# Reordering the hand-written schedule around the second batch's scores, reads and turns

## The chip, the cores and the metric

The kernel runs on one core of a Trainium2 chip. The metric is the device time of one execution in microseconds. TensorE (PE) multiplies matrices into PSUM; VectorE (DVE), ScalarE (ACT) and GpSimd (POOL) do the element-wise work; SyncE (SP) only issues transfers. Lines of the profile name these engines by the short forms, and L12 is line 12 of the kernel.

## The reference

Two blocks follow one another. The first is a cross attention between a long sequence `x` (8 batches, 8 heads, 512 rows, 64 columns) and 32 state rows per head, in both directions. The second takes the 544 rows of each batch, 512 wide, adds the real part of a two-dimensional Fourier transform, normalises the rows and runs a two-layer network over them with a residual. Some 5,000 matrix rows pass through the two layers (512 to 2048 to 512).

```python
def _attn_ref(x, state):
    scores = scale * np.matmul(x, state.transpose(0, 1, 3, 2))
    a = np.exp(scores - max); a /= a.sum(-1)      # 512 x 32 per head
    xread = np.matmul(a, state)
    scores2 = scale * np.matmul(state, x.transpose(0, 1, 3, 2))
    a2 = softmax(scores2)                         # 32 x 512 per head
    sread = np.matmul(a2, x)
    return np.concatenate([xread, sread], axis=2)

def _moe_ref(x, w_ch1, w_ch2):
    mixed = np.real(np.fft.fft(np.fft.fft(x, axis=1), axis=2))
    u = x + mixed
    un = (u - mean(u)) / np.sqrt(var(u) + 1e-06)
    return u + np.maximum(un @ w_ch1, 0.0) @ w_ch2
```

(Softmax and mean are shortened here.)

## The kernel before

**Order of work.** The engines run in parallel, but each goes through its own instructions in the order in which the program issues them. Nothing reorders them: the program text is the schedule. For batches 0 and 1 that order is written out by hand, call by call (lines 1111 to 1239); from batch 2 on, a function `weave` spreads lists of steps over a stage by fractions. The change touches the hand-written part alone.

**Steps of one batch.** A batch b passes through these, and the schedule interleaves several batches:

- `attend(b)` gives the attention. *Scores* (`scores(i)`, L422, then the exponential E on ScalarE, L427) are made twice, for two halves of the rows. *Turned scores* (`turn_scores(g)`, L434, copied to ET on ScalarE, L435) follow. In the schedule these four are `s1[0..3]` for batch 1, `s2[0..3]` for batch 2, `s3[0..3]` for batch 3.
- *Reads* follow: `r1` for batch 1, `R` for batch 2. R[0] is the first row read, with a copy XT of 32 rows made on GpSimd (L501); R[1] folds that copy on GpSimd (`fold_low`, `fold_low_again`); R[2], R[4] and R[6] are the other row reads (`xread`, L447 on TensorE, then a reciprocal and a multiply on VectorE, L455 and L456); R[3] is the per-head read (`sread_by_head`, L467 on TensorE, L470 and L474 on VectorE). L474 writes the rows that the copy XT is made from. The row reads share a PSUM buffer, psX, of which there is one. R[6] to R[8] go on to the folds on VectorE that feed the transform.
- `transform(b)` gives the Fourier part: `over_s` over the rows (L774, copied to G on ScalarE, L775), `over_d` over the columns (L670, L671), `add` (L675; `add_sums`, L793, for batch 0), `centre` with the statistics of each row (L337, L339) and the centred copy `ub` (L831 on ScalarE; `centre_sums`, L808 to L814, for batch 0), and `turn_u`, which turns `ub` into the tile `unT` that layer 1 reads (L842 on TensorE, L843 the copy). For b = 0 and 1 the turn runs on TensorE, for later batches by a transfer. `T` holds these steps for batch 2. There are four pieces (k, r) per batch.
- A *root* (L343, L344, GpSimd) makes the reciprocal deviation of one piece. For batches 0 and 1 roots are collected in `first_roots` and started by hand: entries 0 and 5 to 7 belong to batch 0, entries 1 to 4 to batch 1. `spread` makes the statistics of a piece of batch 0, for the root.
- `layer1(b)` multiplies by the first weights: `L` for batch 0 is 16 quarter steps (L927, four steps per column group of unT, in the order of the four turns), `L1` for batch 1 is 16 steps (L917) that each read all of unT. The activation goes to hT on ScalarE (L929, L919).
- `layer2(b)` is 16 steps of four matmuls (L982), `M` for batch 0. Four steps make one output tile; the fourth adds the residual on VectorE (`store`, L949), which needs that tile's root, and sends it out. `M1` is M[7] and those after it, so M1[1] is M[8].

**PSUM buffers.** Besides psX there are three `psQ` buffers (scores, turned scores, turned `ub`, the transform's results) and three `psF` buffers (the results of both layers). A buffer is taken in the order of the program and is free when the engine that empties it has done so.

**Other queues.** `cast_x(3)` (L148) on GpSimd converts the rows of batch 3, loaded as `xs` by SyncE (L145), and transfers turn them (`turned[3]`). GpSimd has this cast, XT's copy, the folds of low rows and the roots in one queue.

Of the kernel before, what the change touches and what calls it, by code (L numbers as in the profile page):

```python
# [30 lines left out]
def kernel(  # L31
# [8 lines left out]
    nc = tc.nc  # L40
    B, H, S, D = x.shape
# [11 lines left out]
    s_dram = nc.dram_tensor("s_dram", (B, H, Ns, D), F32, kind="Internal")  # L53
# [55 lines left out]
    def states(lo, hi):  # L109
        return stf[:, lo:hi] if lo < 3 else stl[:, lo - 3:hi - 3]  # L110

    def load_state(lo, hi, src=state):
        nc.sync.dma_start(
            out=states(lo, hi).rearrange("p b g d -> p (b g) d"),
            in_=src[lo:hi].rearrange("b (g hh) j d -> (hh j) (b g) d", hh=4),
        )
# [4 lines left out]
    def load_x(b):  # L121
        xs = xs_of[b] if b in xs_of else wk.tile([128, 4 * dm], F32, name="xs", tag="xs")
        xs_of[b] = xs
        v = xs.rearrange("p (i h d) -> p i h d", i=4, d=D)
        xb = x[b].rearrange("h s d -> s h d")
        row = v[15:32:16, 3]
        parts = [
            (v[:, 0], xb[1:129]),
            (v[:, 1], xb[144:272]),
            (v[:, 2], xb[273:401]),  # L130
            (v[32:128, 3], xb[416:512]),
            (v[0:15, 3], xb[129:144]),
            (v[16:31, 3], xb[401:416]),
            (row, xb[0:273:272]),
        ]
        if b == 0:
            for queue, n in ((nc.sync, None), (nc.scalar, 2), (nc.sync, 3), (nc.scalar, 0), (nc.sync, 4), (nc.sync, 5), (nc.sync, 6),
                             (nc.sync, 1)):
                if n is None:
                    load_state(0, 1)  # L140
                else:
                    queue.dma_start(out=parts[n][0], in_=parts[n][1])
            return
        for o, rows in parts:
            nc.sync.dma_start(out=o, in_=rows)  # L145

    def cast_x(b, copy=nc.gpsimd.tensor_copy, lo=0, hi=4):
        copy(xin_bufs[b % 2][:, lo:hi, 1:513], xs_of[b].rearrange("p (i c) -> p i c", i=4)[:, lo:hi])  # L148
# [203 lines left out]
    first_roots = []  # L352
# [5 lines left out]
    turned = {}  # L358
# [546 lines left out]
    def layer1(key):  # L905
        low = isinstance(key, tuple)
        n = 128 if low else 512
        hT = wk.tile([128, FC, n], BF16, name="hTL" if low else "hT", tag="hTL" if low else "hT", bufs=1 if low else 2)
        h_of[key] = hT
        per = 512 // n  # L910

        def step(i):
            ph = psF.tile([128, 512], F32, name="ph", tag="c")
            for f in range(per * i, per * i + per):
                o = (f % per) * n
                for c in range(DC):
                    nc.tensor.matmul(ph[:, o:o + n], lhsT=w1[:, c, f * 128:(f + 1) * 128], rhs=un_of[key][:, c, :],  # L917
                                     start=(c == 0), stop=(c == DC - 1))
            nc.scalar.activation(hT[:, per * i:per * i + per, :].rearrange("p a b -> p (a b)"), ph, AF.Relu,  # L919
                                 scale=-1.0 / 512 if key == 0 else -1.0 if key in flipped else 1.0)  # L920

        def quarter_step(i, r):
            ph = psF.tile([128, 512], F32, name="ph", tag="c")
            for f in range(4 * i, 4 * i + 4):
                o = 128 * (f % 4)
                for c in range(DC):
                    nc.tensor.matmul(ph[:, o:o + 128], lhsT=w1[:, c, f * 128:(f + 1) * 128],  # L927
                                     rhs=un_of[key][:, c, 128 * r:128 * r + 128], start=(c == 0), stop=(c == DC - 1))
            nc.scalar.activation(hT[:, 4 * i:4 * i + 4, 128 * r:128 * r + 128], ph.rearrange("p (a b) -> p a b", b=128),  # L929
                                 AF.Relu, scale=-1.0 / 512 if key == 0 else -1.0 if key in flipped else 1.0)  # L930

        if key == 0:
            return [lambda i=i, r=r: quarter_step(i, r) for r in range(4) for i in range(FC // 4)]
        return [lambda i=i: step(i) for i in range(FC // per)]
# [82 lines left out]
    begin, terms_of, low_of, out_of, keep_low, over_d, add_sums, centre_sums, turn_u, spread, done, keep_middle = transform(0)  # L1017
# [87 lines left out]
    L, M = layer1(0), layer2(0)  # L1105
    over_s1, over_d1, add1, centre1, turn_u1, done1 = transform(1)
# [20 lines left out]
    turned[2, 0]()  # L1127
    load_state(3, 4, s_dram)
    turn_u(0, 1)
    copies1[0]()  # L1130
    copies1[1]()
    copies1[2]()
    add_sums(0, 0)
    centre_sums(0, 0)
    warm(4)
    L[0]()
    s1[0]()
    s1[1]()
    L[1]()
    turn_u(0, 0)  # L1140
    add_sums(1, 1)
    add_sums(1, 0)
    L[2]()
    s1[2]()
    s1[3]()
    centre_sums(1, 1)
    L[3]()
    L[4]()
    r1[0]()
    r1[1]()  # L1150
    r1[2]()
    nc.gpsimd.tensor_copy(gate, xs_of[2].rearrange("p (i c) -> p i c", i=4)[:, :, 0])
    second_weights(2, 4)
    clear_state(4, B)
    L[5]()
    r1[4]()
    r1[3]()
    centre_sums(1, 0)
    turn_u(1, 1)
    L[6]()  # L1160
    r1[5]()
    L[7]()
    r1[6]()
    r1[7]()
    nc.gpsimd.tensor_copy(gate, XQs[1].rearrange("p (g j c) -> p g j c", g=2, j=4)[:, 1, 3, 0:4])
    for i in range(4):
# [4 lines left out]
    turned[2]()  # L1171
    load_x(3)
    turn_in_dram(4, B)
    L[8]()
    L[9]()
    turn_u(1, 0, nc.scalar.copy)
    spread(0, 1)
    state_ones(2, B)
    L[10]()
    L[11]()  # L1180
    L[12]()
    L[13]()
    over_s1(0)
    over_s1(1)
    L[14]()
    over_s1(2)
    over_s1(3)
    keep_middle()
    L[15]()
    over_d1(0)  # L1190
    add1(0, 1)
    M[0]()
    centre1(0, 1)
    over_d1(1)
    add1(0, 0)
    M[4]()
    centre1(0, 0)
    add1(1, 1)
    M[1]()
    turn_u1(0, 1, nc.scalar.copy)  # L1200
    centre1(1, 1)
    M[5]()
    add1(1, 0)
    turn_u1(0, 0, nc.scalar.copy)
    centre1(1, 0)
    M[2]()
    M[6]()
    turn_u1(1, 1)
    done()
    first_roots[0]()  # L1210
    M[3]()
    spread(0, 0)
    turn_u1(1, 0)
    first_roots[5]()
    done1()
    l2, scores_first = M, scores_next
    for b in range(1, B + 1):
        reads_next = reads_after
        l2, l2_now = (layer2(b), [l2[7]] + l2[8:]) if b == 1 else (layer2(b) if b < B else [], l2)
        early, until, start = {2: (7, 0.25, 0.22), 3: (3, 0.13, 0.1)}.get(b, (0, 0, 0.08))  # L1220
        l2_now = l2_now + (layer2(("L", b // 4)) if b in (3, 7) else [])
        streams = [(l2_now[:early], 0, until), (l2_now[early:], until + 0.02 if early else 0, 1)]
        if b == 1:
            M1, L1, R, T, s2 = l2_now, layer1(1), reads_next, transform(2), scores_first
            scores_next, reads_after = attend(3)
            s3 = scores_next
            def spreads():
                spread(1, 1)
                spread(1, 0)
                for root in first_roots[6:8] + first_roots[1:5]:  # L1230
                    root()

            for step in (M1[0], spreads, M1[1], M1[2], s2[0], s2[1], L1[0], M1[3], s2[2], s2[3], L1[1], lambda: cast_x(3), turned[3], L1[2],
                         lambda: load_state(4, B, s_dram), lambda: load_x(4), R[0], L1[3], R[1], R[3], L1[4], R[2], L1[5], M1[4], R[4],
                         L1[6], M1[5], R[6], L1[7], R[7], L1[8], M1[6], R[8], L1[9], L1[10], M1[7], T[0], T[1], L1[11], T[2], T[3],
                         L1[12], T[4], L1[13], T[5], s3[0], L1[14], T[6], s3[1], L1[15], T[7], M1[8], T[8], s3[2], s3[3], T[9], T[10],
                         T[11], lambda: state_blocks(4, B, nc.gpsimd.tensor_copy)):
                step()
            continue
        if b < B:  # L1240
            streams.append((layer1(b), start, 1))
        if b + 1 < B:
            reads, mix = {2: ((0.1, 0.45), (0.57, 0.88)), 3: ((0.03, 0.4), (0.5, 0.86))}.get(b, ((0, 0.375), (0.47, 0.85)))
            streams.append((reads_next, *reads))
            streams.append((transform(b + 1), *mix))
        if b + 2 < B:
            scores_next, reads_after = attend(b + 2)
            streams.append(([lambda: (cast_x(b + 2), turned[b + 2]())], 0.2, 0.2))
            streams.append((scores_next, 0.5, 1))
        if b + 3 < B:  # L1250
            streams.append(([lambda: load_x(b + 3)], 0.35, 0.35))
        if b in (3, 7):
            streams.append((low_rows(b // 4), 0.02, 0.2))
            streams.append((layer1(("L", b // 4)), 0.36, 0.8))
        weave(*streams)
# [30 lines left out]
```

The softmax here doesn't subtract the row's maximum and nothing guards it: scores larger than these inputs give would overflow.

## Time and profile before

Three runs gave 302.44, 302.45 and 302.70 us (median 302.45). The profiled execution has a span of 300.8 us, with the full TensorE clock throughout.

| engine | busy us | share of the span |
|---|---|---|
| PE | 286.6 | 95% |
| PE weight loads | 164.1 | 55% |
| DVE | 176.9 | 59% |
| ACT | 139.4 | 46% |
| POOL | 90.9 | 30% |

A line of a timeline gives start, duration, engine, line, operation, what is written and read, shape and count; in brackets the idle time of the engine just before it, and what ended that. A matmul's duration is modelled and overlaps with the next; four matmuls of 128x512 start 0.86 us apart in all. The table of stretches gives busy time per engine, and in brackets the number of instructions.

### The profile page before, as it was taken

To read this page: it belongs to the slowest core of one execution; us is meant where nothing else is said; L and a number is where in the kernel's file an instruction comes from. 1 tells how busy PE (TensorE), PEld (TensorE's weight loads), DVE (VectorE), ACT (ScalarE), POOL (GpSimd) and SP (SyncE) were. 2 spreads that over 40 slices of the span, in tenths; PEclk is the share of its full clock that TensorE was granted. 3 is DMA by queue.
4 is the path that set the end of the run, shared out by engine and by line. 5 is a ranking of instruction groups with operands and counts; after the bars stand their busy time and mean duration, and the time that the engine had idled before them with its cause. 6 is when DMAs were issued, how large, how long until landed. Compare 5 with 4: busy or idle time off the path is not lost.

```text
span 300.8 us, 6004 instructions
## 1 busy us (share of the span) xinstructions
PE 286.6 (95%) x2288; PEld 164.1 (55%) x2319; DVE 176.9 (59%) x441; ACT 139.4 (46%) x260; POOL 90.9 (30%) x227
## 2 busy tenths in 40 slices
PE   5998999979899999999999999999999999999995
PEld 5788894535544555466544554455444544555443
DVE  8855888457858487645748394756568474000022
ACT  6887575626734661355433534354524433334200
POOL 6764841670391044401333032502240131000000
PEclk9999999999999999999999999999999999999999
DMA  9999983958563932585343774254332033500355
GB/s 157 198 204 191 164 147 77 202 117 161 127 150 81 208 88 72 123 163 118 85 93 89 155 142 131 46 105 89 88 79 64 35 89 86 123 13 25 95 121 135
DMA packets 110824, 34.86 MB, mean 116 GB/s; under 512 B 101980, under 2 KB 106332, under 8 KB 110796
## 3 DMA queue, kind: packets, MB, share of 16 engines
q1 hardware_dynamic: 100076, 28.72, 44.3%
q0 software_dynamic: 4224, 4.19, 8.9%
q10 hardware_dynamic: 6496, 1.57, 2.6%
q8 instruction: 18, 0.29, 0.4%
q14 instruction: 10, 0.08, 0.1%
HBM read 22.41 MB, written 14.02 MB: 121 GB/s over the span
## 4 chain that ended last, share of the span: by engine, by line
PE 70%; DVE 8%; DMA 6%; SPq 5%; POOL 4%; issue 3%; ACT 2%; POOLq 0%; DVEq 0%; ACTq 0%
PE po L982 31%; PE ph L917 30%; SPq L145 4%; DMA s_dram<-in_state_dram 3%; PE gp L774 2%; DMA gen<-s_dram 2%; POOL xin L148 1%; SPq L388 1%; PE po L974 1%; DMA r_dram<-ot 1%; PE yp L671 1%; PE yp L670 1%; DVE U L675 1%; DVE st L337 1%; PE xrp L447 1%
## 5 line engine op out<-in xcount | busy, mean ns | idle before, releaser
L982 PE MATMUL po<-w,hT 128*128 128x512 bf16 x481 | 121.3, 379 | 1.3 <-issue 0.5
L919 ACT ACTIVATE hT<-ph 128x512 bf16<-128x512 f32 x112 | 66.9, 597 | 112.9 <-PE ph L917 111.8
L917 PE MATMUL ph<-unT,w 128*128 128x512 bf16 x432 | 111.7, 379 | 0.9 <-DVE ot L949 0.3
L917 PEld LDWEIGHTS <-w 128*128 128x128 bf16 x576 | 50.3, 98 | 46.0 <-issue 0.9
L982 PEld LDWEIGHTS <-hT 128*128 128x128 bf16 x496 | 46.9, 98 | 47.6
L949 DVE SCALAR_TENSOR_TENSOR ot<-po,rstd,U 128x512 f32<-128x512 f32 (+2 forms) x33 | 24.1, 731 | 51.0 <-PE po L982 45.6
L778 POOL COPY GL<-G 128x128 bf16<-128x128 bf16 x7 | 2.0, 291 | 74.0 <-ACT G L775 74.0
L337 DVE BATCH_NORM_STATS2 st<-U 128x6 f32<-128x512 f32 x32 | 21.8, 682 | 0.1
L343 POOL TENSOR_TENSOR rstd<-mv,epst 128x1 f32<-128x1 f32 x34 | 6.8, 200 | 48.1 <-DVE mv L339 48.1
L675 DVE TENSOR_TENSOR U<-yp,XR 128x512 f32<-128x512 f32 x14 | 9.5, 681 | 20.0 <-PE yp L671 20.0
L344 POOL TENSOR_TENSOR rstd<-rstd,mhalf 128x1 f32<-128x1 f32 x34 | 19.8, 583 | 2.7
L927 PE MATMUL ph<-unT,w 128*128 128x128 bf16 x256 | 16.1, 219 | 0.3 <-DVE unT L843 0.3
L775 ACT CAST G<-gp 128x288 bf16<-128x288 f32 x28 | 12.9, 482 | 4.9 <-PE gp L774 4.9
L927 PEld LDWEIGHTS <-w 128*128 128x128 bf16 x256 | 14.9, 98 | 0.5 <-issue 0.4
L929 ACT ACTIVATE hT<-ph 128x512 bf16<-128x512 f32 x16 | 9.4, 598 | 5.1 <-PE ph L927 5.0
L148 POOL CAST xin<-xs 128x2048 bf16<-128x2048 f32 (+1 forms) x9 | 11.7, 1319 | 0.1
L501 POOL COPY XT<-XR 32x514 bf16<-32x514 bf16 x7 | 4.2, 604 | 21.6 <-DVE XR L456 19.9
L833 DVE TENSOR_SCALAR ub<-U,mv 128x512 bf16<-128x512 f32 x20 | 10.3, 513 | 0.7
L427 ACT ACTIVATE E<-esp 128x512 bf16<-128x512 f32 x14 | 8.2, 595 | 4.4 <-PE esp L422 4.3
L456 DVE TENSOR_TENSOR XR<-xrp,rs 128x512 bf16<-128x512 f32 x14 | 9.7, 695 | 0.5
L456 DVE TENSOR_TENSOR XF<-xfp,rs 128x512 bf16<-128x512 f32 x14 | 9.7, 692 | 0.5
L447 PEld LDWEIGHTS <-ET 128*128 128x128 bf16 x56 | 5.1, 98 | 9.0 <-DVE XF L456 3.0
(240 smaller groups left out, 377.8 us busy)
## 6 DMA issues: line engine op xcount, KB each, us to landing
xs<-in_x_dram SPq DMA_DIRECT2D x22, 256.0 KB, 4.7
w<-in_moe_w_ch_dram POOLq DMA_DIRECT2D x8, 512.0 KB, 8.8
out_dram<-ot SPq DMA_DIRECT2D x15, 256.0 KB, 3.6
r_dram<-ot SPq DMA_DIRECT2D x14, 256.0 KB, 2.1
out_dram<-r_dram SPq DMA_DIRECT2D x14, 256.0 KB, 3.5
xs<-in_x_dram SPq DMA_DIRECT2D x8, 192.0 KB, 4.5
xs<-in_x_dram ACTq DMA_DIRECT2D x2, 256.0 KB
l_dram<-ot SPq DMA_DIRECT2D x2, 256.0 KB
```

Of the source, the lines that this page charges most:

```text
L145: nc.sync.dma_start(out=o, in_=rows)
L148: copy(xin_bufs[b % 2][:, lo:hi, 1:513], xs_of[b].rearrange("p (i c) -> p i c", i=4)[:, lo:hi])
L337: nc.vector.bn_stats(st6, u)
L344: nc.gpsimd.tensor_tensor(rstd, rstd, mhalf, op=ALU.pow)
L456: nc.vector.tensor_tensor(ov, in0=p[ps, :, 0:256].rearrange("p g (h d) -> p g h d", d=D), in1=rs[ps].unsqueeze(3).to_broadcast([n, 2, 4, D ...
L675: nc.vector.tensor_add(u.rearrange("p (k r) -> p k r", r=2), p.rearrange("p (r k) -> p k r", r=2)[:, 0:u.shape[1] // 2, :], x.rearrange("p ...
L775: nc.scalar.copy(G[:, j, :].rearrange("p (i q) -> p q i", q=2), p[:, 0:NM].rearrange("p (q i) -> p q i", q=2))
L917: nc.tensor.matmul(ph[:, o:o + n], lhsT=w1[:, c, f * 128:(f + 1) * 128], rhs=un_of[key][:, c, :], start=(c == 0), stop=(c == DC - 1))
L919: nc.scalar.activation(hT[:, per * i:per * i + per, :].rearrange("p a b -> p (a b)"), ph, AF.Relu, scale=-1.0 / 512 if key == 0 else -1.0 ...
L927: nc.tensor.matmul(ph[:, o:o + 128], lhsT=w1[:, c, f * 128:(f + 1) * 128], rhs=un_of[key][:, c, 128 * r:128 * r + 128], start=(c == 0), st ...
L949: nc.vector.scalar_tensor_tensor(ot[:, cols], in0=po_of[i][:, 0:cols.stop - cols.start], scalar=rstd, in1=u[:, cols], op0=ALU.mult, op1=AL ...
L982: nc.tensor.matmul(po_of[i], lhsT=h_of[key][:, f, i * 128:(i + 1) * 128], rhs=w2[:, f, :], start=(f == 0), stop=(f == FC - 1))
```

## The change

The change moves calls and leaves every instruction as it is. It has five parts.

1. Batch 0's `add_sums(0, 0)` and `centre_sums(0, 0)` come ahead of the copies for batch 1. Batch 1's scores come behind two steps of layer 1 (L[0], L[1]) and the turn of piece (0, 0), where they stood behind one step.
2. All later steps L come one place earlier against the scores, reads and turns of batch 1, and `turn_u(1, 0)` moves ahead of the last read `r1[7]`. Batch 1's `over_s`, `over_d` and turns come one step later against L and M. This keeps TensorE supplied while the scores wait for their operands.
3. M[7] and M[8] move ahead of the last two turns of batch 1, `turn_u1(1, 1)` and `turn_u1(1, 0)`; root 5 is started before them.
4. For batch 2 the row read R[2] comes ahead of the per-head read R[3], and the four roots of batch 1 move behind R[1], so that GpSimd and VectorE reach what the row reads need sooner.
5. The scores of batch 3, s3[0] and s3[1], come ahead of T[5] and T[6], which hold centrings.

```diff
--- before.py
+++ after.py
@@ -1127,40 +1127,42 @@
     turned[2, 0]()
     load_state(3, 4, s_dram)
     turn_u(0, 1)
+    add_sums(0, 0)
+    centre_sums(0, 0)
     copies1[0]()
     copies1[1]()
     copies1[2]()
-    add_sums(0, 0)
-    centre_sums(0, 0)
     warm(4)
     L[0]()
+    L[1]()
+    turn_u(0, 0)
     s1[0]()
     s1[1]()
-    L[1]()
-    turn_u(0, 0)
     add_sums(1, 1)
     add_sums(1, 0)
     L[2]()
+    L[3]()
     s1[2]()
     s1[3]()
     centre_sums(1, 1)
-    L[3]()
     L[4]()
+    L[5]()
     r1[0]()
     r1[1]()
     r1[2]()
     nc.gpsimd.tensor_copy(gate, xs_of[2].rearrange("p (i c) -> p i c", i=4)[:, :, 0])
     second_weights(2, 4)
     clear_state(4, B)
-    L[5]()
+    L[6]()
     r1[4]()
     r1[3]()
     centre_sums(1, 0)
     turn_u(1, 1)
-    L[6]()
+    L[7]()
     r1[5]()
-    L[7]()
+    L[8]()
     r1[6]()
+    turn_u(1, 0, nc.scalar.copy)
     r1[7]()
     nc.gpsimd.tensor_copy(gate, XQs[1].rearrange("p (g j c) -> p g j c", g=2, j=4)[:, 1, 3, 0:4])
     for i in range(4):
@@ -1171,47 +1173,47 @@
     turned[2]()
     load_x(3)
     turn_in_dram(4, B)
-    L[8]()
     L[9]()
-    turn_u(1, 0, nc.scalar.copy)
     spread(0, 1)
     state_ones(2, B)
     L[10]()
     L[11]()
     L[12]()
     L[13]()
+    L[14]()
     over_s1(0)
     over_s1(1)
-    L[14]()
+    L[15]()
     over_s1(2)
     over_s1(3)
     keep_middle()
-    L[15]()
+    M[0]()
     over_d1(0)
     add1(0, 1)
-    M[0]()
+    M[4]()
     centre1(0, 1)
     over_d1(1)
     add1(0, 0)
-    M[4]()
+    M[1]()
     centre1(0, 0)
     add1(1, 1)
-    M[1]()
+    M[5]()
     turn_u1(0, 1, nc.scalar.copy)
     centre1(1, 1)
-    M[5]()
+    M[2]()
     add1(1, 0)
+    M[6]()
     turn_u1(0, 0, nc.scalar.copy)
     centre1(1, 0)
-    M[2]()
-    M[6]()
-    turn_u1(1, 1)
     done()
     first_roots[0]()
     M[3]()
     spread(0, 0)
+    first_roots[5]()
+    M[7]()
+    turn_u1(1, 1)
+    M[8]()
     turn_u1(1, 0)
-    first_roots[5]()
     done1()
     l2, scores_first = M, scores_next
     for b in range(1, B + 1):
@@ -1227,13 +1229,17 @@
             def spreads():
                 spread(1, 1)
                 spread(1, 0)
-                for root in first_roots[6:8] + first_roots[1:5]:
+                for root in first_roots[6:8]:
                     root()
 
-            for step in (M1[0], spreads, M1[1], M1[2], s2[0], s2[1], L1[0], M1[3], s2[2], s2[3], L1[1], lambda: cast_x(3), turned[3], L1[2],
-                         lambda: load_state(4, B, s_dram), lambda: load_x(4), R[0], L1[3], R[1], R[3], L1[4], R[2], L1[5], M1[4], R[4],
+            def roots():
+                for root in first_roots[1:5]:
+                    root()
+
+            for step in (spreads, M1[2], s2[0], s2[1], L1[0], M1[3], s2[2], s2[3], L1[1], lambda: cast_x(3), turned[3], L1[2],
+                         lambda: load_state(4, B, s_dram), lambda: load_x(4), R[0], L1[3], R[1], roots, M1[4], R[2], L1[4], R[3], L1[5], R[4],
                          L1[6], M1[5], R[6], L1[7], R[7], L1[8], M1[6], R[8], L1[9], L1[10], M1[7], T[0], T[1], L1[11], T[2], T[3],
-                         L1[12], T[4], L1[13], T[5], s3[0], L1[14], T[6], s3[1], L1[15], T[7], M1[8], T[8], s3[2], s3[3], T[9], T[10],
+                         L1[12], T[4], L1[13], s3[0], T[5], L1[14], s3[1], T[6], L1[15], T[7], M1[8], T[8], s3[2], s3[3], T[9], T[10],
                          T[11], lambda: state_blocks(4, B, nc.gpsimd.tensor_copy)):
                 step()
             continue
```

## The prediction

> **What bounds the kernel now.** I read the page first, for the share of each engine, then the busy time of each engine by stretches of ten microseconds, then the timeline of TensorE over the part that the change touches (19 to 85 us), and last the other engines' timelines at each gap. Times of events are microseconds from the start of the span, in the profile of the kernel before.
>
> ```profile
> PE 286.6 (95%) x2288; PEld 164.1 (55%) x2319; DVE 176.9 (59%) x441; ACT 139.4 (46%) x260; POOL 90.9 (30%) x227
> ```
>
> TensorE is busy for 95% of 300.8 us. The change removes no matmul, so only TensorE's idle time can be won: 14.2 us, most of it in the opening and the tail. In the stretches (total, then busy time of PE, weight loads, DVE, ACT, POOL, then clock, DMA share, GB/s) the changed part shows two holes, 1.96 us and 1.10 us:
>
> ```profile
> 50.00:60.00 10.00, 9.87 (x103) 5.17 (x103) 5.73 (x15) 5.77 (x12) 4.93 (x14) 1.00 0.85 175
> 60.00:70.00 10.00, 8.04 (x40) 3.77 (x40) 6.28 (x14) 3.18 (x6) 5.49 (x10) 1.00 0.53 108
> 70.00:80.00 10.00, 9.89 (x77) 5.74 (x77) 7.61 (x21) 6.60 (x13) 1.75 (x5) 1.00 0.89 174
> 80.00:90.00 10.00, 8.90 (x80) 4.41 (x81) 5.96 (x16) 4.63 (x11) 7.99 (x17) 1.00 0.56 133
> ```
>
> TensorE's timeline names them. Brackets hold the idle time just before the instruction and who ended it:
>
> ```profile
> 23.98 0.35 PE L422 MATMUL esp<-sT,xT 128*128 128x64 bf16 x6 [0.49 <-DVE xT L411]
> 24.78 0.39 PE L422 MATMUL esp<-sT,xT 128*128 128x64 bf16 x8 [0.45 <-DVE U L793]
> ...
> 34.28 0.40 PE L447 MATMUL xrp<-stb,ET 128*128 128x260 bf16 x2 [0.39 <-DVE XF L456]
> ...
> 61.81 1.03 PE L982 MATMUL po<-w,hT 128*128 128x512 bf16 x3
> 64.75 0.40 PE L447 MATMUL xfp<-stb,ET 128*128 128x260 bf16 x2 [1.91 <-DVE XF L456]
> ...
> 80.78 0.25 PE L434 MATMUL eTp<-ident,E 128*128 128x128 bf16 x2 [0.75 <-ACT E L427]
> ...
> 84.35 0.28 PE L447 MATMUL xrp<-stb,ET 128*128 128x260 bf16 x1 [0.29 <-ACT ET L435]
> ```
>
> The large one, 1.91 us, is a chain over three engines. GpSimd:
>
> ```profile
> 59.29 0.19 POOL L343 TENSOR_TENSOR rstd<-mv,epst 128x1 f32<-128x1 f32 x1
> 59.56 0.55 POOL L344 TENSOR_TENSOR rstd<-rstd,mhalf 128x1 f32<-128x1 f32 x1
> 60.06 1.89 POOL L148 CAST xin<-xs 128x2048 bf16<-128x2048 f32 x1
> 61.90 0.61 POOL L501 COPY XT<-XR 32x514 bf16<-32x514 bf16 x1
> ```
>
> and VectorE:
>
> ```profile
> 59.59 0.16 DVE L470 RECIPROCAL rcs<-sums 128x2 f32<-128x2 f32 x1
> 62.54 1.19 DVE L474 TENSOR_TENSOR XR<-srp,rcs 32x128 bf16<-32x128 f32 x4 [2.79 <-POOL XT L501]
> 63.76 0.21 DVE L455 RECIPROCAL rs<-xfp 128x8 f32<-128x8 f32 x1
> 64.00 0.69 DVE L456 TENSOR_TENSOR XF<-xfp,rs 128x512 bf16<-128x512 f32 x1
> ```
>
> GpSimd computes six roots back to back (two instructions each, 55.35 to 60.11), then the cast of batch 3, then copies XT. L474 overwrites the rows that this copy reads, so it waits 2.79 us. Behind it on VectorE stand the reciprocal and multiply that empty the only psX buffer (R[2], the row read), and TensorE needs that buffer for the next row read, R[4].
>
> **What the Trainium skill says.** "PSUM — Partial Sum Buffer", section "Engine vs sequencer instructions": ScalarE, VectorE and GpSimd queues are strict first-in first-out, and matmuls start in program order. The trace agrees: R[2]'s matmuls had been issued at 60.73, and VectorE touched it only at 63.76, right after L474. "Perfetto Trace Analysis", section "Optimization Strategy": look for the gaps of the contended engine and for what blocks each. That is how the list above was made. "SBUF — State Buffer", section "SBUF: two separate sides": GpSimd and some VectorE operations take turns on a shared port. The trace fits that at one place: centre_sums(1, 0) on VectorE took 0.92 us at 32.13, with GpSimd busy, against 0.48 for the same shape at 24.96.
>
> **The change, part by part.**
>
> *Late part: row read and roots (the 1.91 us).* Four roots leave the front of the queue: 4 x 0.79 us (55.35 to 56.14 is one period) = 3.1 us, so GpSimd would be free at about 57.0. The cast then waits for its data. The landing records put the last of the seven parts of xs at 58.06. The cast moves from 60.06 to 58.1 at best, and XT's copy ends near 60.6 instead of 62.5. Besides, R[2] now stands ahead of the per-head read R[3], so psX is emptied before VectorE reaches L474 at all. On the new order TensorE passes L1[4] (0.86), R[3] (0.37) and L1[5] (0.86) between R[2] and R[4], 2.1 us, and VectorE needs about 1.7 of it: a store (0.67) and R[2]'s 0.9. Then rcs, L474 and R[4]'s own emptying (0.15 + 1.2 + 0.9) must be through before R[6], which comes 0.22 + 2 x 0.86 after R[4]: about 0.4 us to spare. I take the whole 1.91 as won. The four roots run after fold_low (3.65 us of GpSimd), and their first reader is a store of batch 1 past 85 us: nothing. *Bounds*: 1.2 if half of these margins fail, 1.91 if none.
>
> *Early part: scores behind two steps.* VectorE runs add_sums(0, 0) and centre_sums(0, 0) (1.60 us, 23.84 to 25.44 now) straight after the copy that ends at 22.3, so to 23.95, and the xT copy (0.69) to 24.65. TensorE runs L[0] and L[1] (0.89 each) from 22.37 to 24.15, turns ub(0, 0) to 24.38, waits 0.33 for xT, then about 0.15 for the psQ buffer that turn_u's copy frees at 25.1; L[2] starts at 25.35, not 26.13. Won: 0.75. Then L[8] comes before r1[6], and it is the first step on the third column group, whose turned tile VectorE copies only after centre_sums(1, 0): about 33.5, against TensorE's arrival at 32.6. That costs 0.9 and hides the old 0.39 wait. r1[7] moves from 34.28 to about 34.9, with L[8] and a turn (1.1 us) already done. The fold that follows it on VectorE shifts by 0.6; over_s1(0) and over_s1(2) arrive at 40.5 and 41.9, when it delivers at 40.35 and 41.85. TensorE is then 0.5 ahead in work, and as M[0] stands ahead of over_d1(0), that starts at 43.45 against 43.01.
>
> *The turn of batch 1: a new wait.* VectorE is busy without a gap from 43.64 to 50.67 on adds and statistics of batch 1, so this chain ends 0.44 later, at 50.67 for the last aggregate. The two gaps of TensorE before turns (0.32 and 0.18, at 47.87 and 51.10) close, and TensorE reaches s2[0] at 53.0 instead of 53.92. But on VectorE M[7]'s store now stands before both unT copies, and it waits for root 5:
>
> ```profile
> 51.86 0.69 DVE L337 BATCH_NORM_STATS2 st<-U 128x6 f32<-128x512 f32 x1
> 52.58 0.18 DVE L339 BATCH_NORM_AGGREGATE mv<-st 128x2 f32<-128x6 f32 x1
> 52.68 0.39 DVE L843 COPY unT<-tp 128x512 bf16<-128x512 bf16 x1
> 53.70 0.75 DVE L949 SCALAR_TENSOR_TENSOR ot<-po,rstd,U 128x512 f32<-128x512 f32 x1 [0.63 <-POOL rstd L344]
> ```
>
> Statistics end to store is 0.94 here (52.76 to 53.70). So: 50.67, store of M[3] 0.67, statistics 0.9, root 0.94, store 0.67, two copies 0.38 each = 54.6. s2[1] waits for a psQ buffer until 54.3, and L1[0], which reads all of unT, starts at 54.65 against 54.39. What the early part won is spent, and 0.26 more. *Bounds*: 0.9 won if this convoy costs nothing, 0.8 lost if every link is a quarter of a microsecond longer.
>
> *Scores of batch 3 ahead of centrings.* E of s3[0] leaves ScalarE before ub(0, 1), so the 0.75 wait at 80.78 goes. I cost it at nothing, because the read of batch 3 that follows waits for ET, and ET stands behind ub(1, 0), which waits for statistics on VectorE (82.33), a chain without a gap from 75.60, begun by over_d(0), which the edit leaves in place. Twelve matmuls later TensorE would stand 0.75 + 0.29 at that read instead. *Bounds*: 0 to 0.75.
>
> Sum: -1.91 + 0.26 = **-1.65 us**. Past 85 us TensorE is the bound (99% busy from 120 to 280), so the shift should reach the end: 302.45 - 1.65 = 300.8.
>
> **Rivals.**
> A. The early convoy is cheaper, or the scores' edit pays: -1.91 - 0.9 = -2.8, or -1.65 - 0.75 = -2.4; 299.7 to 300.1. For it: the visible TensorE waits shrink. Against it: both rest on VectorE chains with no gap.
> B. A small gain: half the hole stays because R[6] or R[4] still meets VectorE behind L474 (margin 0.4 us), or the convoy costs 1 us: 301.3 to 301.9.
> C. Slower: the convoy before L1[0] grows to 1.3 us (all that TensorE had won ahead, plus 0.4), L474 takes the same time late enough to hold R[6] for 1 us, and the later cast of xs columns (0.6 us) delays transposes: -1.91 + 1.3 + 1.0 + 0.6 = +1.0, 303.4. Against it: XT is copied two microseconds earlier by two independent edits.
>
> **How the numbers follow.** Forecast (300.2 to 301.3) 0.60, A 0.17, B 0.10, within 0.2% (301.85 to 303.05) 0.03, C 0.10. Range 299.7 to 301.7 leaves some 2 in 10 out. Faster 0.86, same 0.04, slower 0.10.
>
> **What would show it.** Right: no idle before R[4] near 63; L474 without a long wait; the cast starting at the landing of xs near 58.5; a gap of about 1 us before s2[1] and L1[0] near 54, with VectorE's store ahead of two copies; a gap near 33 before L[8]; none at eTp of batch 3 but about 1 us at the read after it. Wrong: if s2[1] finds its buffer early, or the read of batch 3 does not wait, it is A; if XT's copy still ends past 62, B or C.

## The result and the profile after

| | median us | lowest to highest | runs |
|---|---|---|---|
| before | 302.57 | 302.44 to 303.27 | 4 |
| changed | 300.57 | 300.40 to 300.60 | 4 |

The ratio is 0.9928, with a 95% interval from 0.9911 to 0.9945: the changed kernel is 2.0 us faster. The forecast was 300.8. A later measurement of both, side by side on one chip, gave 302.45 and 300.59 (ratio 0.9940, 0.9928 to 0.9953).

The page of the changed kernel: TensorE has as many matmuls as before and 0.9 us less modelled busy time, in a span that is 2.0 us shorter (298.8).

```profile
PE 285.7 (96%) x2288; PEld 163.3 (55%) x2319; DVE 176.6 (59%) x441; ACT 139.5 (47%) x260; POOL 91.8 (31%) x227
```

The stretches of ten microseconds, with the columns as before:

```profile
50.00:60.00 10.00, 9.06 (x70) 5.06 (x70) 5.89 (x14) 5.91 (x13) 2.74 (x7) 1.00 0.80 156
60.00:70.00 10.00, 9.95 (x80) 4.83 (x80) 8.33 (x21) 4.42 (x8) 8.89 (x17) 1.00 0.55 127
...
80.00:90.00 10.00, 8.86 (x73) 4.12 (x73) 5.33 (x15) 3.68 (x8) 8.54 (x15) 1.00 0.68 145
```

The hole between 60 and 70 is gone (busy 9.95 of 10, from 8.04). A smaller one is new between 50 and 60 (9.06, from 9.87). The hole between 80 and 90 is as large as it was (8.86, from 8.90). TensorE's timeline shows where the waits stand now:

```profile
22.26 1.95 PE L927 MATMUL ph<-unT,w 128*128 128x128 bf16 x32 [0.29 <-DVE unT L843]
...
33.38 1.07 PE L927 MATMUL ph<-unT,w 128*128 128x128 bf16 x16 [0.78 <-DVE unT L843]
...
54.17 0.39 PE L422 MATMUL esp<-sT,xT 128*128 128x64 bf16 x8 [0.84 <-DVE unT L843]
54.50 1.02 PE L917 MATMUL ph<-unT,w 128*128 128x512 bf16 x4
...
62.78 0.39 PE L447 MATMUL xfp<-stb,ET 128*128 128x260 bf16 x2
...
64.73 0.39 PE L447 MATMUL xrp<-stb,ET 128*128 128x260 bf16 x2
...
81.80 0.28 PE L447 MATMUL xrp<-stb,ET 128*128 128x260 bf16 x1 [0.79 <-ACT ET L435]
82.37 0.28 PE L447 MATMUL xrp<-stb,ET 128*128 128x260 bf16 x1 [0.29 <-ACT ET L435]
```

R[4] at 62.78 has no bracket any more. There are new waits before L[8] (33.38) and before s2[1] (54.17), and the wait for E that was at 80.78 is replaced by one for ET at 81.80, before the read. VectorE at the old hole, with R[2]'s emptying now ahead of L474, and nothing to wait for at L474:

```profile
61.54 0.69 DVE L456 TENSOR_TENSOR XF<-xfp,rs 128x512 bf16<-128x512 f32 x1
62.15 0.15 DVE L470 RECIPROCAL rcs<-sums 128x2 f32<-128x2 f32 x1
62.44 1.19 DVE L474 TENSOR_TENSOR XR<-srp,rcs 32x128 bf16<-32x128 f32 x4
```

GpSimd, two roots where there were six, then the cast, which waits for its data, and the copy XT:

```profile
56.41 0.55 POOL L344 TENSOR_TENSOR rstd<-rstd,mhalf 128x1 f32<-128x1 f32 x1
59.47 1.89 POOL L148 CAST xin<-xs 128x2048 bf16<-128x2048 f32 x1 [2.50 <-DMA xs<-in_x_dram]
61.30 0.60 POOL L501 COPY XT<-XR 32x514 bf16<-32x514 bf16 x1
```

And VectorE before L1[0], the convoy that the prediction named, one instruction held behind another (end of the statistics, 0.94 us of waiting for root 5, the store, then both copies of unT):

```profile
51.92 0.18 DVE L339 BATCH_NORM_AGGREGATE mv<-st 128x2 f32<-128x6 f32 x1
53.04 0.75 DVE L949 SCALAR_TENSOR_TENSOR ot<-po,rstd,U 128x512 f32<-128x512 f32 x1 [0.94 <-POOL rstd L344]
53.71 0.74 DVE L843 COPY unT<-tp 128x512 bf16<-128x512 bf16 x2
```

Where the 2.0 us came from, read at four marks of TensorE in both traces. Three marks of the kernel before stand in these lines, the fourth in the prediction:

```profile
22.37 1.05 PE L927 MATMUL ph<-unT,w 128*128 128x128 bf16 x16 [0.29 <-DVE unT L843]
...
54.39 1.03 PE L917 MATMUL ph<-unT,w 128*128 128x512 bf16 x4
...
66.71 0.39 PE L447 MATMUL xrp<-stb,ET 128*128 128x260 bf16 x2
```

| mark | before | changed | difference |
|---|---|---|---|
| L[0] starts | 22.37 | 22.26 | -0.11 (the opening, which the change leaves alone) |
| L1[0] starts | 54.39 | 54.50 | +0.11 |
| R[6] starts | 66.71 | 64.73 | -1.98 |
| second half of batch 3's first read | 84.35 | 82.37 | -1.98 |

So the early part costs 0.22, the late part wins 2.09, the scores of batch 3 win nothing, and from there on the difference stays to the end. The opening, up to L[0], differs by up to 0.35 us between the executions traced here (22.25 to 22.60), so differences of this size are read from marks in the trace and not from the times.

### The profile page after: what moved, and what is told of

The parts are those of the page before. It is cut to its first block, busy times and chain, and to the rows that moved or that the text cites. A ratio compares the mean times of both kernels' runs of the same rounds, so it can differ in the third digit from the quotient of the medians.

```text
span 298.8 us, 6004 instructions
## 1 busy us (share of the span) xinstructions
PE 285.7 (96%) x2288; PEld 163.3 (55%) x2319; DVE 176.6 (59%) x441; ACT 139.5 (47%) x260; POOL 91.8 (31%) x227
## 3 DMA queue, kind: packets, MB, share of 16 engines
q10 hardware_dynamic: 6496, 1.57, 2.6%
## 4 chain that ended last, share of the span: by engine, by line
PE 82%; DVE 12%; ACT 2%; issue 2%; POOL 1%; DVEq 0%; POOLq 0%; ACTq 0%
PE po L982 33%; PE ph L917 32%; PE ph L927 5%; PE gp L774 3%; DVE st L337 2%; DVE U L675 2%; PE yp L670 1%; PE yp L671 1%; PE po L974 1%; DVE ot L949 1%; PE xrp L447 1%; PE eTp L434 1%; PE esp L422 1%; PE gp L717 1%; PE xfp L447 1%
## 5 line engine op out<-in xcount | busy, mean ns | idle before, releaser
L344 POOL TENSOR_TENSOR rstd<-rstd,mhalf 128x1 f32<-128x1 f32 x34 | 20.8, 611 | 2.7
L455 DVE RECIPROCAL rs<-xrp 128x8 f32<-128x8 f32 x14 | 2.9, 206 | 14.2 <-PE xrp L447 14.2
```

The lines of the kernel that those rows point to most:

```text
L344: nc.gpsimd.tensor_tensor(rstd, rstd, mhalf, op=ALU.pow)
```

## The experiments

The diffs are shortened: calls of several lines are joined, and `lambda:` is left out. The first four runs take the change apart and ran on one chip (before: 302.71).

**Only the order of the reads**, in the kernel before:

```diff
-R[0], L1[3], R[1], R[3], L1[4], R[2], L1[5], M1[4], R[4],
+R[0], L1[3], R[1], M1[4], R[2], L1[4], R[3], L1[5], R[4],
```

> The kernel before with one edit: the row read R[2] stands ahead of the per-head read R[3], the six roots stay ahead of the cast. Theory 1 (either edit alone frees the row-read buffer): L474 still waits for XT's copy until about 62.5 us, but R[2] has been emptied by then, R[4] starts near 62.8 and R[6] near 64.8 instead of 66.7; about -2.0 us, 300.5. Theory 2 (the roots in front of the cast are the cause, and the order of the reads only decides which of them waits): the wait moves to R[6], and no more than 0.5 us is won, 302.0 or more.

Measured: 300.66 us (ratio 0.9923, 0.9893 to 0.9952). L474 still waits for XT's copy (0.32 us here, 2.79 before), and R[2] has been emptied by then:

```profile
61.66 0.69 DVE L456 TENSOR_TENSOR XF<-xfp,rs 128x512 bf16<-128x512 f32 x1
62.75 1.19 DVE L474 TENSOR_TENSOR XR<-srp,rcs 32x128 bf16<-32x128 f32 x4 [0.32 <-POOL XT L501]
```

```profile
64.96 0.40 PE L447 MATMUL xrp<-stb,ET 128*128 128x260 bf16 x2
```

From L[0] (22.60 here) to R[6] it is 42.36 us, and was 44.34: 1.98 less. This edit alone wins nearly the whole, so theory 2 falls: the roots were not the only way out. The edit, like the change, also moves the layer 2 step M1[4] ahead of R[2]. That step alone was not run; in the trace before, R[2]'s emptying stands behind L474, and M1[4] would leave it there.

**Only the roots**, in the kernel before:

```diff
-for root in first_roots[6:8] + first_roots[1:5]: root()      # in spreads
+for root in first_roots[6:8]: root()
-R[0], L1[3], R[1], R[3],
+R[0], L1[3], R[1], roots, R[3],        # roots: first_roots[1:5]
```

> The kernel before with one edit: four of the six roots stand behind R[1], the reads keep their order. Theory 1: the cast starts at the landing of the rows of batch 3 near 58.1, XT's copy ends near 60.6, L474 follows at once, psX is emptied near 62.8, and R[4] waits 0.2 us at most; about -1.9 us, 300.6. Theory 2: the same, and here it is the whole of the gain. Theory 3 (only the swap matters, since the cast is bound by the landing and not by the roots): less than 0.7 us is won, 301.8 or more.

Measured: 301.17 us (ratio 0.9950, 0.9923 to 0.9976). The runs spread widely, eleven of thirteen from 300.53 to 302.41. The cast starts 0.2 us after the rows have landed (58.39 by the landing records; the bracket names a matmul that ended in the same moment), and the copy ends 1.5 us sooner, but R[4] still waits:

```profile
58.61 1.89 POOL L148 CAST xin<-xs 128x2048 bf16<-128x2048 f32 x1 [1.75 <-PE xrp L447]
60.44 0.60 POOL L501 COPY XT<-XR 32x514 bf16<-32x514 bf16 x1
```

```profile
63.29 0.40 PE L447 MATMUL xfp<-stb,ET 128*128 128x260 bf16 x2 [0.55 <-DVE XF L456]
```

The roots alone win about three quarters of it by the times (1.5 us), and 1.36 us from L[0] (22.27) to R[6] (65.25): better than theory 3, short of theory 1. The cast started 0.5 us later than theory 1 had it, as the rows landed 0.3 us later than before and it follows them by 0.2; that is most of what is missing.

**Both edits of the late part, nothing else**: the two diffs above together.

> The kernel before with both edits of the late part (R[2] ahead of R[3], four roots behind R[1]) and nothing of the early part, nor of the scores of batch 3. Theory 1: the hole of TensorE before R[4] goes whole, 2.1 us with the overlap that the bracket's 1.91 leaves out, and the early part's loss of 0.2 is not paid: 300.3 to 300.5, a little faster than the changed kernel. Rival (the early part carries a share of the gain): 301 or more.

Measured: 300.53 us (ratio 0.9915, 0.9882 to 0.9948).

```profile
62.58 0.38 PE L447 MATMUL xfp<-stb,ET 128*128 128x260 bf16 x2
...
64.52 0.39 PE L447 MATMUL xrp<-stb,ET 128*128 128x260 bf16 x2
```

R[6] starts at 64.52, 0.2 earlier than in the changed kernel. The late part is the whole gain; that this kernel beats the changed one by 0.2 is seen in the marks only, not in the times.

**Only the early part**: the changed kernel with `spreads`, the order of the reads and the scores of batch 3 as before.

> The kernel before with the early edits alone (scores of batch 1 behind two steps, steps L one place earlier, transforms one step later, M[7] and M[8] ahead of the last turns). Theory 1: L1[0] starts 0.1 to 0.3 us later than before, the roots and the cast stay where they are, so the hole before R[4] ends at about the same time, 64.75: within 0.3 us of the kernel before, 302.2 to 302.8. Rival (the shorter waits of TensorE near 24 us are a gain of 0.5 to 0.9 us that lasts): 301.6 to 302.0.

Measured: 302.76 us (ratio 0.9992, 0.9973 to 1.0012). The shorter waits near 24 us are there, and then TensorE waits at the same place:

```profile
64.87 0.40 PE L447 MATMUL xfp<-stb,ET 128*128 128x260 bf16 x2 [1.78 <-DVE XF L456]
```

L[0] started at 22.40 and R[6] at 66.83, against 22.37 and 66.71 before. The rival, that the early gain lasts, falls.

The next four ran on another chip (before: 302.58).

**The scores of batch 3 put back** behind the centrings, in the changed kernel:

```diff
-L1[13], s3[0], T[5], L1[14], s3[1], T[6],
+L1[13], T[5], s3[0], L1[14], T[6], s3[1],
```

> The changed kernel with its last part undone: s3[0] and s3[1] stand behind T[5] and T[6] again, as before. Theory 1 (the edit only moves a wait): the wait of 0.75 us for E before the turned scores of batch 3 comes back, the wait for ET before the read after it shrinks by as much, the second matmul of that read starts at the same 82.4 us, and the time is the changed kernel's, 300.4 to 300.7. Rival (the edit pays): 0.5 to 0.75 us slower, about 301.2.

Measured: 301.00 us (300.59 to 301.85; ratio to before 0.9931, 0.9908 to 0.9953), on a chip on which the changed kernel did not run, so the times do not separate the two. The trace does:

```profile
79.11 0.25 PE L434 MATMUL eTp<-ident,E 128*128 128x128 bf16 x2 [0.75 <-ACT E L427]
...
82.69 0.28 PE L447 MATMUL xrp<-stb,ET 128*128 128x260 bf16 x1 [0.29 <-ACT ET L435]
```

The wait for E is back and the first wait of the read is gone. From L[0] to the second half of the read it is 60.13 us here (22.56 to 82.69) and 60.11 in the changed kernel: the edit moves 0.75 us of waiting and wins none up to this read.

**The store of M[7] behind the turns**, in the changed kernel:

```diff
-M[7](); turn_u1(1, 1); M[8](); turn_u1(1, 0); done1()        # then spreads, M1[2], s2[0]
+M[8](); turn_u1(1, 1); M[9](); turn_u1(1, 0); M[7](); done1()   # then spreads, s2[0]
```

> The changed kernel with M[7], and so its store with the wait for root 5, behind the last two turns of batch 1 (M[8] and M[9] take its place ahead of them). Theory 1 (this store on VectorE ahead of both copies of unT is what holds s2[1] and L1[0]): L1[0] starts near 53.4 us instead of 54.5; then R[6] meets VectorE behind L474, whose copy XT ends at 61.9 as the rows of batch 3 land no earlier, so that some 0.7 of the 1.1 us lasts: 299.7 to 300.0. Rival (the turn is bound by the statistics of batch 1, not by the store): L1[0] stays after 54.0 and the time within 0.2 us of the changed kernel.

Measured: 300.39 us in the median, spread from 299.48 to 301.52 (ratio 0.9916, 0.9889 to 0.9943). VectorE now makes the copies first:

```profile
52.03 0.72 DVE L843 COPY unT<-tp 128x512 bf16<-128x512 bf16 x2
53.23 0.75 DVE L949 SCALAR_TENSOR_TENSOR ot<-po,rstd,U 128x512 f32<-128x512 f32 x1 [0.48 <-PE po L982]
```

```profile
53.42 1.03 PE L917 MATMUL ph<-unT,w 128*128 128x512 bf16 x4
```

L1[0] starts at 53.42 and R[6] at 63.65, both 1.1 us earlier than in the changed kernel. The new wait of the change was this store. That all of it lasted to R[6] in this execution, where 0.7 was expected, has its reason in the rows of batch 3: the cast could start at 58.83. But the execution traced is one of the two shortest of ten (299.48). The median missed the expected 299.7 to 300.0. It lies only 0.2 us below the changed kernel's, measured on other chips; that is the rival's number for the time, while its number for L1[0] fell. How much of the 1.1 us a typical execution keeps is not shown by this run.

**L[8] behind r1[6] and the turn**, on top of the last kernel:

```diff
-L[8](); r1[6](); turn_u(1, 0, nc.scalar.copy); r1[7]()
+r1[6](); turn_u(1, 0, nc.scalar.copy); L[8](); r1[7]()
```

> The kernel of the run before this one, with L[8] moved behind r1[6] and turn_u(1, 0), so that TensorE does not stand 0.8 us before L[8]. Theory 1: r1[7] starts 0.7 us earlier, near 34.2, and everything up to L1[0] with it, but R[6] is then held by L474 and the copy XT (cast bound by the landing of the rows of batch 3): no more than 0.2 us better than the kernel before it. Rival (TensorE's idle time alone counts): 0.7 us better, about 299.1.

Measured: 300.25 us (298.96 to 301.70; ratio 0.9909, 0.9876 to 0.9942). r1[7] starts at 34.30 instead of 34.95 and s2[0] at 52.30 instead of 52.95; then the gain stops, where it was expected to (the spread of the times is too wide to tell the two kernels apart):

```profile
61.51 1.19 DVE L474 TENSOR_TENSOR XR<-srp,rcs 32x128 bf16<-32x128 f32 x4 [0.55 <-POOL XT L501]
```

R[6] waits for VectorE behind it and starts at 63.72, against 63.65.

**XT's copy ahead of the cast**, on top of that:

```diff
-L1[1], cast_x(3), turned[3], L1[2], load_state(4, B, s_dram), load_x(4), R[0], L1[3],
+L1[1], L1[2], R[0], cast_x(3), turned[3], load_state(4, B, s_dram), load_x(4), L1[3],
```

> The kernel of the run before this one, with the cast of batch 3 and its turn behind R[0], so that GpSimd copies XT before it casts. Theory 1: XT's copy no longer waits for the landing of batch 3, L474 and R[6] are not held, and the whole of the two savings shows: 1.4 to 1.8 us better than the changed kernel, 298.8 to 299.2. Rival (the later cast delays the transfers of batch 3 and its scores wait for them): 299.5 to 300.5.

Measured: 299.22 us (ratio 0.9885, 0.9846 to 0.9925). GpSimd copies 2.6 us earlier, and the cast is not late by it:

```profile
58.29 0.60 POOL L501 COPY XT<-XR 32x514 bf16<-32x514 bf16 x1 [2.45 <-DVE XR L456]
58.86 1.90 POOL L148 CAST xin<-xs 128x2048 bf16<-128x2048 f32 x1
```

R[6] starts at 63.17.

The last four ran on the chip of the first four, at a later time (before: 302.45). **The changed kernel once more** came first, as a measure for the others:

> The changed kernel once more, on the chip of the three runs after it, so that they can be set against it: 300.4 to 300.7, as measured first.

Measured: 300.59 us (300.58 to 300.80).

**The order of the reads put back** in the changed kernel, the roots left behind R[1]:

```diff
-R[1], roots, M1[4], R[2], L1[4], R[3], L1[5], R[4],
+R[1], roots, R[3], L1[4], R[2], L1[5], M1[4], R[4],
```

> The changed kernel with one edit undone: the per-head read R[3] stands ahead of the row read R[2] again; the four roots stay behind R[1]. In the changed kernel the rows of batch 3 landed at 59.2 us, and XT's copy ended at 61.9. Theory 1 (here the order of the reads carries the gain, as the cast is bound by the landing): L474 follows the copy, psX is emptied near 64.0, R[4] waits for 1.0 to 1.3 us by the bracket, and the time is about 1.2 us above the changed kernel, 301.6 to 301.9. Rival (moving the roots is enough in this kernel too): within 0.3 us of it.

Measured: 300.90 us (ratio to before 0.9952, 0.9939 to 0.9964), 0.3 above the changed kernel and not 1.2: a miss, and the rival's number. The expectation took the landing of batch 3's rows from the one trace at hand, 59.2 us. Here, and in the changed kernel's own second trace, the landing records have 58.1 and 58.2. So XT's copy ended at 60.8, and L474 waited 0.98:

```profile
60.82 1.19 DVE L474 TENSOR_TENSOR XR<-srp,rcs 32x128 bf16<-32x128 f32 x4 [0.98 <-POOL XT L501]
```

With rows that land as early as this the roots alone are nearly enough; the order of the reads is what makes the changed kernel indifferent to a landing up to 59.2: R[6] starts at 64.73 in both of its traces, with the rows at 59.2 and at 58.2. It has its limit, as the next trace shows.

**ET ahead of the last centring**, in the changed kernel:

```diff
-T[7], M1[8], T[8], s3[2], s3[3],
+T[7], M1[8], s3[2], s3[3], T[8],
```

> The changed kernel with the turned scores s3[2] and s3[3] of batch 3 ahead of T[8], so that ScalarE makes ET before the last centring. Theory 1 (the scores' edit wins nothing because ET stands behind that centring): both waits before the read of batch 3, 0.8 and 0.3 us, go; the first step of layer 1 of batch 2 then waits for the transfer of unT, which landed at 86.0 us and left 0.6 us to spare, so that some 0.5 us lasts: 299.9 to 300.2. Rival A: the whole 1.1 us lasts, 299.5. Rival B: the later centring delays unT's transfers, and nothing lasts or it is slower.

Measured: 299.80 us (299.72 to 301.04; ratio to before 0.9911, 0.9896 to 0.9926), 0.8 below the changed kernel. Both waits before the read are gone:

```profile
81.43 0.39 PE L447 MATMUL xrp<-stb,ET 128*128 128x260 bf16 x2
```

The profiled execution was the 301.04 one, in which the rows of batch 3 landed at 60.4. With rows as late as that the order of the reads no longer covers it all:

```profile
63.09 1.19 DVE L474 TENSOR_TENSOR XR<-srp,rcs 32x128 bf16<-32x128 f32 x4 [0.48 <-POOL XT L501]
```

R[6] starts 2.22 us after R[4] here (63.09 to 65.31), and 1.95 in the changed kernel. The trace also shows what stands behind the two waits before the read, the transfer of unT, which landed at 86.96:

```profile
87.10 1.02 PE L917 MATMUL ph<-unT,w 128*128 128x512 bf16 x3 [1.25 <-DMA unT<-ub]
```

So the reason given for the scores' edit holds: ET behind ub(1, 0) was the wait that took over. How much of the 1.1 us lasts depends on that transfer, which landed at 86.0 and at 85.4 in the two traces of the changed kernel, and lies between theory 1 and rival A; no trace shows a typical execution of this kernel.

**The best version again**, the store last, L[8] later, and XT's copy ahead of the cast:

> The kernel with the store last, L[8] behind r1[6] and XT's copy ahead of the cast, once more beside the changed kernel on one chip: 1.2 to 1.7 us below it, 298.9 to 299.3.

Measured: 298.95 us (298.86 to 299.13; ratio to before 0.9885, 0.9871 to 0.9898), beside 300.59 for the changed kernel: 1.6 us faster than it, 3.5 than before. R[6] starts at 63.07, also 1.7 us earlier. The three edits together keep what the first of them did not keep alone.

## Why the prediction was right, step by step

- *Late part, -1.91 forecast: right, and larger.* The marks give 2.09. The term was read from the bracket, which counts from the modelled end of the last matmul. That end is 1.03 us after its group of four starts, while the next group can start after 0.86; the bracket leaves out these 0.17. The start of R[4] less the start of the four matmuls ahead of it (64.75 - 61.81 = 2.94) less 0.86 is 2.08, the number that was won. The prediction read two other gaps, those before the turns at 47.87 and 51.10, in this better way.
- *The reason for it: half right.* The prediction gave the earlier cast and the new order of the reads as two independent edits. They are two ways out of the same wait: by the marks the order alone won 1.98, the roots alone 1.36, both together 2.08. The cast at 58.1 to 58.5 was wrong for the first trace (59.47, rows at 59.23) and right for the second (58.39); XT's copy ended at 61.9 and 60.8, where 60.6 was forecast. The margin at R[6] was 0.14 us and not 0.4: XF was written by 64.59 and R[6] started at 64.73. The prediction's own terms give no more than 0.1 to 0.2. A store of 0.67 and 0.9 make 1.57 and not 1.7; with the 2.25 after them VectorE is through at 3.8 to 3.95, and R[6] comes at 2.1 + 1.94 = 4.04. That the hole went whole was a closer thing than the prediction said, and with rows at 60.4 a part came back.
- *Scores behind two steps: right.* L[2] at 25.17 (forecast 25.35), the wait before L[8] 0.78 by the bracket (0.9), r1[7] at 34.94 (34.9), over_d1(0) at 43.40 (43.45). The wait of 0.33 for xT did not show; the only one there is 0.21 before the second half of the scores, for the buffer that unT's copy frees.
- *The turn of batch 1: right.* s2[0] at 52.94 (53.0), s2[1] at 54.17 (54.3), L1[0] at 54.50 (54.65), and the run with the store last shows that the store is the cause. The net cost is 0.22 between L[0] and L1[0], against 0.26.
- *Scores of batch 3: right.* The 0.75 us wait moved to the read (0.79 there), and ET first brings a gain where the scores' edit brings none.
- *Rivals.* A fell on both of its halves; of B, R[6]'s margin held, barely; of C, the cast of xs columns did come 0.65 us later (42.11 against 41.46), but the loads of batch 3 moved by 0.2 us in the second trace. In the first they were 1.1 later, and 0.8 of that is a wait of GpSimd for state rows, which the second trace does not have. The new order of the reads hides both.

The sum was -1.65 and the measured difference at the marks -1.98: 0.18 is the bracket, 0.04 the convoy, and 0.11 the opening, which the change leaves alone.

## What to carry to other kernels

When a single buffer is emptied by an in-order engine, look at what stands ahead of the emptying in that engine's queue: here putting it ahead of an instruction that waits for a third engine was worth more (1.98 us) than hurrying that engine (1.36), and it kept its worth when the third engine's data landed 1 us later. Shorter waits ahead of a later common wait were worth nothing: follow each saving to the next place where another engine's chain arrives last. Where a store that waits for a small result stands ahead of copies that the next matmuls need, put the copies first; layer 1 started 1.1 us earlier here, and the time followed in full only when the copy XT no longer stood behind the cast.

## What the runs showed of the hardware

- In these traces a bracket before a matmul is short by the overlap of modelled ends: 0.17 us behind groups of four 128x512 matmuls (1.03 modelled, the next group 0.86 after the start).
- The seven loads of batch 3's rows were complete at 58.1 to 60.4 us in four executions of kernels with the same order up to there (58.1, 58.2, 59.2, 60.4), with openings that differ by 0.15 us at most. GpSimd's cast started 0.21 to 0.24 us after the last landing in each of them. The loads themselves took about the same time: the last landing came 2.5 to 2.7 us after the last issue. What varied was the issue, 55.5 to 57.7. In three of the traces it can be followed back: these loads stand on SyncE behind turns that wait for GpSimd, and GpSimd converts the state rows `gen` first, which landed at 43.6, 45.1 and 46.4 us where batch 3's rows landed at 58.2, 59.2 and 60.4. This is read from the traces; no edit tested it. GpSimd at this place in the first two of them:

```profile
44.31 1.26 POOL L168 CAST stb<-gen 32x128 bf16<-32x128 f32 x4
```

```profile
45.17 1.27 POOL L168 CAST stb<-gen 32x128 bf16<-32x128 f32 x4 [0.81 <-DMA gen<-s_dram]
```

- The last two of batch 1's four roots, moved beside VectorE's folds, took 0.27 to 0.38 us and 1.01 us for their two instructions (66.49 to 69.3) instead of 0.19 and 0.55; the first two did not. The prediction had met the like from the other side at 32.1, where VectorE was the slower one. It costs nothing here, as nobody waits for these roots.
